# Two feature tiles per sigmoid, gate product, rounding and low part in the first mixer, with the second product four feature tiles behind

## Chip, cores and metric

The kernel runs as one program on 1 core of one Trainium2 chip. The metric is the device time of one execution in microseconds (us). A core has TensorE (PE; its weight loads are listed apart as PEld), VectorE (DVE), ScalarE (ACT), GpSimd (POOL) and SyncE (SP, which here only issues DMAs).

## What is computed

Three stages follow each other (4 batches, sequence length 768, model width 384 = 8 heads of 48):

```python
# attention: a state decayed in each step, per batch and head
cur = einsum('bhd,bhe->bhde', u * k_t, v_t)
y_t = einsum('bhd,bhde->bhe', r_t, state + cur)
state = w * state + einsum('bhd,bhe->bhde', k_t, v_t)
# first mixer: 384 -> 1024 -> 384, convolution of 3 taps over the sequence
h = maximum(x @ w_in, 0)
conv = sum over k of conv_w[k] * h shifted by k - 1
x = (h * sigmoid(conv)) @ w_out
# second mixer: 384 -> 1536 -> 384, with a norm in front
xn = (x - mean) / sqrt(var + 1e-6) * g_ln
out = x + maximum(xn @ w_ch1, 0) @ w_ch2
```

All operands are float32. Each large product is made of three products of rounded high parts (type fp32r) and low parts: high by high, high by low, low by high.

## The kernel before

**Attention** goes over 24 tiles of 128 sequence positions (`attn_tile`, line 341, and `state_update`, line 380). Its generator is advanced by `step()` (line 728). It delivers the transposed high and low parts `xh`, `xl` that the first mixer reads. The DMAs of a tile's inputs `rk`, `kt` and `rv` are issued by `load_tile` three tiles ahead, into buffers that earlier tiles have left. DVE multiplies `rk` by a table (line 347) before PE may use it.

**First mixer** (`mixer1`, line 539): 8 blocks of T = 384 positions, each with NF1 = 8 feature tiles of 128 features, so 64 feature tiles in all. For each of them `moe1_up` (line 463) makes:
- the first product, 9 matmuls of 386 columns into a `psm` bank (two banks);
- on ACT a relu into `h` (line 471) and the middle tap into `c` (line 472); on DVE the two outer taps into `c` (line 474, two instructions);
- for the feature tile before it (`prev`): `gate`, that is the sigmoid on ACT (line 454) and the product h * c on DVE (line 455), and then `gate_split`, the rounding to the high part `gh` on ACT (line 460) and the low part `gl` on DVE (line 461).

So sigmoid, product, rounding and low part are one instruction of 128x384 each per feature tile: 64 of each in the kernel.

**The second product** (`down`, line 441; 9 matmuls of 384 columns into three `acc` banks) is queued by `queue_down` and run by `pump(n)` until at most n are left in the queue. `LAG` is 3. In `mixer1` a feature tile's second product is queued one tile late and `pump(LAG - 1)` leaves two, so PE runs it right behind the first product three feature tiles on. The queue reaches over the end of a block: the last three second products of a block run in the next one, and those of the last block in the second mixer. After a block's eighth second product ACT empties the three `acc` banks (`evacuate`, line 496), and `spill` writes them to DRAM.

**Around it**: `before1` and `after1` (lines 762 and 768) put the decoding of the weights (`need`, `wdo`) and the attention's `step()` into the feature loop. A weight's high and low parts are made out of raw words by ACT, POOL and DVE. `need(wo_job[f - LAG + 1])` calls for the rows of the second weight that are to come.

**Second mixer** (`mixer2`, line 555): 6 blocks of 512 positions, 12 feature tiles each, with relu and low part only, and `pump(LAG)`.

**Order of the work**: the order on PE is the order in which the program is written (`InOrder`, line 67); so is the order of the weights' decoding among itself. The instructions of `v_`, `a_`, `g_` and the loads on SP are put in order, and the on-chip buffers put in place, when the program is built, by a planner with a timing model of its own (`_TILE`, line 851). Each engine then runs its instructions in that fixed order, and waits on semaphores.

Of the kernel before, what the change touches and what calls it, by code (L numbers as in the profile page):

```python
# [8 lines left out]
F32 = mybir.dt.float32  # L9
F32R = mybir.dt.float32r  # L10
I32 = mybir.dt.int32
AF = mybir.ActivationFunctionType
ALU = mybir.AluOpType
# [7 lines left out]
NF1 = FF1 // 128  # L21
NF2 = FF2 // 128
C = 128
TPB = S // C
NT = B * TPB
T = 384
TT = T // C
# [8 lines left out]
LAG = 3  # L36
# [12 lines left out]
def body(ctx, tc, r, k, v, w, u, w_in, conv_w, w_out, g_ln, w_ch1, w_ch2, rkT, krv, small, out):  # L49
# [6 lines left out]
    mp = ctx.enter_context(tc.tile_pool(name="mp", bufs=2))  # L56
# [6 lines left out]
    v_ = nc.vector  # L63
# [29 lines left out]
    gl = smallt[:, 3 * NP:]  # L93
# [347 lines left out]
    def down(acc, gh, gl_, wh, wl, f, nf):  # L441
        for t in range(len(acc)):
            sl = slice(t * 128, t * 128 + 128)
            for q, (a, x) in enumerate(((gh, wh), (gh, wl), (gl_, wh))):
                pe.matmul(acc[t], lhsT=a[:, sl], rhs=x, start=(f == 0 and q == 0),
                          stop=(f == nf - 1 and q == 2))
# [5 lines left out]
    def gate(st):  # L452

        a_.activation(out=st["c"], in_=st["c"], func=AF.Sigmoid)  # L454
        v_.tensor_tensor(out=st["c"], in0=st["h"][:, 1:T + 1], in1=st["c"], op=ALU.mult)  # L455

    def gate_split(st):
        st["gh"] = mp.tile([128, T], F32R, tag="gh", name="gh", bufs=LAG + 1)
        st["gl"] = mp.tile([128, T], F32R, tag="gl", name="gl", bufs=LAG + 1)
        a_.activation(out=st["gh"], in_=st["c"], func=AF.Copy)  # L460
        v_.tensor_tensor(out=st["gl"], in0=st["c"], in1=st["gh"].bitcast(F32), op=ALU.subtract)  # L461

    def moe1_up(x, f, prev):
        ps = ps_m.tile([128, 512], F32, tag="m", name="psm")
        mm3(ps[:, 0:T + 2], [wih[:, kt] for kt in range(KT)], [wil[:, kt] for kt in range(KT)], x[0], x[1], slice(f * 128, f * 128 + 128), slice(0, T + 2))
        if prev is not None:
            gate(prev)
        st = {}
        h = st["h"] = mp.tile([128, T + 2], F32, tag="h", name="h", bufs=3)
        c = st["c"] = mp.tile([128, T], F32, tag="c", name="c", bufs=3)  # L470
        a_.activation(out=h, in_=ps[:, 0:T + 2], func=AF.Relu)
        a_.activation(out=c, in_=h[:, 1:T + 1], func=AF.Copy, scale=cw[:, 1, f:f + 1])  # L472
        for tap, o in ((0, 0), (2, 2)):
            v_.scalar_tensor_tensor(out=c, in0=h[:, o:o + T], scalar=cw[:, tap, f:f + 1], in1=c,  # L474
                                    op0=ALU.mult, op1=ALU.add)
        if prev is not None:
            gate_split(prev)
        return st

    def moe2_up(xn, f, cols):  # L480
        ps = ps_m.tile([128, 512], F32, tag="m", name="psm")
        a, f0 = divmod(f * 128, WN)
        mm3(ps[:, 0:cols], c1h[a], c1l[a], xn[0], xn[1], slice(f0, f0 + 128), slice(0, cols))
        st = {}
        gh = st["gh"] = mp.tile([128, T2], F32R, tag="rh", name="rh", bufs=LAG + 1)
        gl_ = st["gl"] = mp.tile([128, T2], F32R, tag="rl", name="rl", bufs=LAG + 1)
        a_.activation(out=gh[:, 0:cols], in_=ps[:, 0:cols], func=AF.Relu)  # L487
        v_.scalar_tensor_tensor(out=gl_[:, 0:cols], in0=ps[:, 0:cols], scalar=0.0, in1=gh[:, 0:cols].bitcast(F32),  # L488
                                op0=ALU.max, op1=ALU.subtract)
        return st  # L490
# [35 lines left out]
    def pump(n):  # L526
        while len(downq) > n:
            downq.pop(0)()

    def queue_down(st, hold, f, nf, wh, wl, then, tiles=TT):  # L530
        def go():
            if f == 0:
                hold.extend(new_acc(tiles))
            down(hold, st["gh"], st["gl"], wh(f), wl(f), f, nf)
            if f == nf - 1:
                then(hold)
        downq.append(go)

    def mixer1(x, then, before=lambda f: None, after=lambda f: None):
        hold, prev = [], None  # L540
        for f in range(NF1):
            before(f)
            st = moe1_up(x, f, prev)
            if prev is not None:
                queue_down(prev, hold, f - 1, NF1, lambda f: woh[:, f, :], lambda f: wol[:, f, :], then)
            prev = st
            after(f)
            pump(LAG - 1)
            after(f)
        before(NF1)  # L550
        gate(prev)
        gate_split(prev)
        queue_down(prev, hold, NF1 - 1, NF1, lambda f: woh[:, f, :], lambda f: wol[:, f, :], then)

    def mixer2(xn, tiles, then, before=lambda f: None, after=lambda f: None):
        hold = []
        for f in range(NF2):
            before(f)
            queue_down(moe2_up(xn, f, tiles * C), hold, f, NF2, lambda f: c2h[f // 2][:, f % 2, :],
                       lambda f: c2l[f // 2][:, f % 2, :], then, tiles)  # L560
            pump(LAG)
            after(f)
# [315 lines left out]
```

## Time and profile before

| | us |
|---|---|
| median of 3 runs | 669.76 |
| lowest and highest of them | 665.53, 671.35 |
| the profiled execution, its own time | 668.53 |
| its span, from first to last instruction | 666.8 |
| PE, DVE, ACT, POOL busy in the span | 629.3, 431.7, 264.3, 135.1 |
| mean granted clock of TensorE, as a share of full speed | 0.976 |

The span lies 1.7 us below its execution's own time, and that time 1.2 us below the median. Busy time of PE is the time in which at least one matmul's record runs; records overlap. On DVE and ACT too the record of an instruction can reach over the start of the next one.

### The profile page before, as it was taken

The page shows a single profiled execution, that of the slowest core. Times are in us where ns is not written, and L with a number is a line of the kernel's source. Part 1 is how long each engine was busy: PE and PEld are TensorE (multiplying, and loading weights), DVE is VectorE, ACT ScalarE, POOL GpSimd, SP SyncE. Part 2 cuts the span into 40 slices and gives each one's busy share as a digit, 9 for nine tenths or more (in the row PEclk, how much of TensorE's full clock was granted, in tenths as well). Part 3 has the DMA queues.
Part 4 walks back from the last instruction along what each step waited for, and adds up shares of the span by engine and source line. Part 5 has one row for each costly group of instructions (what it writes and reads, how often), then busy time and mean ns, then how long its engine had stood idle before and what let it go on. Part 6 is the DMA issues. An engine that isn't in the chain of part 4 may idle for free.

```text
span 666.8 us, 11692 instructions
## 1 busy us (share of the span) xinstructions
PE 629.3 (94%) x4782; PEld 574.1 (86%) x4782; DVE 431.7 (65%) x772; ACT 264.3 (40%) x518; POOL 135.1 (20%) x142
## 2 busy tenths in 40 slices
PE   5879689999989899999999999999999999999996
PEld 4769579889879898899998999999999999999996
DVE  7887999999999998988788852422422422421211
ACT  3356656455654565566665521221211121121110
POOL 5374642230321213011007510100100100100000
PEclk9978799999989899999999999999999999999999
DMA  8663616235254434102043301101100200200101
GB/s 275 201 211 109 218 41 211 87 101 173 74 161 132 138 102 132 43 2 83 14 167 115 110 1 48 47 1 56 40 1 23 72 1 13 83 1 1 47 1 52
DMA packets 25294, 56.50 MB, mean 85 GB/s; under 512 B 2961, under 2 KB 15378, under 8 KB 25234
## 3 DMA queue, kind: packets, MB, share of 16 engines
q1 hardware_dynamic: 25234, 55.68, 26.3%
q8 instruction: 39, 0.64, 0.4%
q14 instruction: 21, 0.17, 0.1%
HBM read 46.24 MB, written 9.44 MB: 83 GB/s over the span
## 4 chain that ended last, share of the span: by engine, by line
PE 62%; DVE 24%; DMA 6%; issue 3%; ACT 3%; POOL 1%; SPq 1%; DVEq 0%; ACTq 0%
PE psm L75 30%; PE acc L75 30%; DVE c L474 6%; DMA rk<-in_rkT_dram 5%; DVE wdec L75 4%; DVE c L455 2%; DVE aT L363 2%; DVE rk L347 2%; DVE gl L461 2%; PE yps L75 1%; PE pxt L75 1%; DVE av L352 1%; DVE kks L249 1%; DVE a L354 1%; DVE xl L372 1%
## 5 line engine op out<-in xcount | busy, mean ns | idle before, releaser
L488 DVE SCALAR_TENSOR_TENSOR rl<-psm,rh 128x512 fp32r<-128x512 f32 x72 | 49.6, 689 | 133.0 <-ACT rh L487 129.5
L487 ACT ACTIVATE rh<-psm 128x512 fp32r<-128x512 f32 x72 | 43.1, 599 | 193.7 <-PE psm L75 190.1
L75 PE MATMUL acc<-c2h,rh 128*128 128x384 f32 x288 | 97.1, 337 | 0.0
L75 PE MATMUL acc<-c2l,rh 128*128 128x384 f32 x288 | 97.0, 337 | 0.0
L75 PE MATMUL acc<-c2h,rl 128*128 128x384 f32 x288 | 97.0, 337 | 0.0
L474 DVE SCALAR_TENSOR_TENSOR c<-h,tables,c 128x384 f32<-128x384 f32 x128 | 87.0, 685 | 7.4 <-ACT c L472 6.8
L75 PE MATMUL psm<-xnh,c1h 128*128 128x512 f32 x216 | 86.6, 401 | 0.0
L75 PE MATMUL psm<-xnh,c1l 128*128 128x512 f32 x216 | 84.9, 393 | 0.0
L75 PE MATMUL psm<-xnl,c1h 128*128 128x512 f32 x216 | 84.6, 392 | 0.0
L75 PE MATMUL psm<-xh,wih 128*128 128x386 f32 x192 | 70.0, 364 | 7.5 <-DVE aT L363 3.2
L75 PE MATMUL acc<-woh,gh 128*128 128x384 f32 x192 | 68.1, 355 | 2.7 <-ACT x L496 2.7
L75 PE MATMUL acc<-wol,gh 128*128 128x384 f32 x192 | 65.8, 343 | 4.2 <-DVE wol L75 4.2
L75 PE MATMUL psm<-xl,wih 128*128 128x386 f32 x192 | 67.4, 351 | 2.4 <-POOL xl L288 2.4
L75 PE MATMUL acc<-woh,gl 128*128 128x384 f32 x192 | 66.1, 344 | 1.8 <-DVE gl L461 1.8
L75 PE MATMUL psm<-xh,wil 128*128 128x386 f32 x192 | 67.3, 351 | 0.5 <-DVE wil L75 0.5
L75 POOL TENSOR_SCALAR wdec<-wdec 128x768 f32<-128x768 f32 (+2 forms) x19 | 55.3, 2911 | 50.8 <-ACT wdec L75 41.3
L511 POOL TENSOR_TENSOR rs<-rs,nhalf 128x1 f32<-128x1 f32 x24 | 15.5, 654 | 230.5 <-DVE rs L510 229.9
L75 PEld LDWEIGHTS acc<-c2l,rh 128*128 128x128 f32 x288 | 54.1, 188 | 3.0
L75 PEld LDWEIGHTS acc<-c2h,rh 128*128 128x128 f32 x288 | 54.1, 188 | 2.8
L75 PEld LDWEIGHTS acc<-c2h,rl 128*128 128x128 f32 x288 | 54.0, 188 | 0.0
L454 ACT ACTIVATE c<-c 128x384 f32<-128x384 f32 x64 | 33.4, 521 | 44.0 <-DVE c L474 43.5
L357 POOL TENSOR_SCALAR_AFFINE_SELECT aT<-a 128x1024 f32<-128x1024 f32 x18 | 29.1, 1617 | 104.0 <-PE yps L75 45.1
(115 smaller groups left out, 1144.2 us busy)
## 6 DMA issues: line engine op xcount, KB each, us to landing
rk<-in_rkT_dram SPq DMA_DIRECT2D x24, 448.0 KB, 5.0
st<-in_moe_w_ch_dram SPq DMA_DIRECT2D x12, 768.0 KB, 5.9
rv<-in_krv_dram SPq DMA_DIRECT2D x18, 448.0 KB, 4.8
kt<-in_krv_dram SPq DMA_DIRECT2D x24, 192.0 KB, 2.8
x_dram<-x SPq DMA_DIRECT2D x24, 192.0 KB, 2.0
x1b<-x_dram SPq DMA_DIRECT2D x24, 192.0 KB, 3.5
out_dram<-x1b SPq DMA_DIRECT2D x24, 192.0 KB, 2.3
st<-in_moe_w_in_dram SPq DMA_DIRECT2D x6, 512.0 KB, 6.1
```

Source lines behind the costliest of these rows:

```text
L75: return lambda *args, **kw: tc.keep_in_program_order(op(*args, **kw))
L249: v_.tensor_tensor(out=kks[:, n % 2, :, :, 0:D], in0=loaded[n][1].unsqueeze(1).to_broadcast([128, 2, H, D]), in1=tku, op=ALU.mult)
L347: v_.tensor_tensor(out=rk, in0=rk, in1=trk, op=ALU.mult)
L357: g_.affine_select(out=aT.rearrange("x q p c -> x (q p) c"), in_=a8.to_broadcast([128, H, C]), compare_op=ALU.is_equal, fill=0.0, base=0, ...
L363: v_.copy_predicated(out=aT[:, q], mask=later.bitcast(I32).unsqueeze(1).to_broadcast([128, NP, C]), data=dps[q])
L454: a_.activation(out=st["c"], in_=st["c"], func=AF.Sigmoid)
L455: v_.tensor_tensor(out=st["c"], in0=st["h"][:, 1:T + 1], in1=st["c"], op=ALU.mult)
L461: v_.tensor_tensor(out=st["gl"], in0=st["c"], in1=st["gh"].bitcast(F32), op=ALU.subtract)
L474: v_.scalar_tensor_tensor(out=c, in0=h[:, o:o + T], scalar=cw[:, tap, f:f + 1], in1=c, op0=ALU.mult, op1=ALU.add)
L487: a_.activation(out=gh[:, 0:cols], in_=ps[:, 0:cols], func=AF.Relu)
L488: v_.scalar_tensor_tensor(out=gl_[:, 0:cols], in0=ps[:, 0:cols], scalar=0.0, in1=gh[:, 0:cols].bitcast(F32), op0=ALU.max, op1=ALU.subtract)
L511: g_.tensor_tensor(out=rs[:, 1:2], in0=rs[:, 0:1], in1=nhalf, op=ALU.pow)
```

## The change

`h`, `c`, `gh` and `gl` become tiles of two feature tiles (`[128, 2, ...]`), three buffers of each (`gh` and `gl` had four of one). Relu and taps still go feature tile by feature tile, into their half. At every even feature tile the pair before it gets one sigmoid, one product, one rounding and one low part of 128x768, and its two second products are queued together. `pump` leaves three in the queue behind an even feature tile and two behind an odd one, so that a second product runs four feature tiles behind its first. `mixer2` is the same but for the form of the call.

```diff
     def gate(st):
 
         a_.activation(out=st["c"], in_=st["c"], func=AF.Sigmoid)
-        v_.tensor_tensor(out=st["c"], in0=st["h"][:, 1:T + 1], in1=st["c"], op=ALU.mult)
+        v_.tensor_tensor(out=st["c"], in0=st["h"][:, :, 1:T + 1], in1=st["c"], op=ALU.mult)
 
     def gate_split(st):
-        st["gh"] = mp.tile([128, T], F32R, tag="gh", name="gh", bufs=LAG + 1)
-        st["gl"] = mp.tile([128, T], F32R, tag="gl", name="gl", bufs=LAG + 1)
+        st["gh"] = mp.tile([128, 2, T], F32R, tag="gh", name="gh", bufs=3)
+        st["gl"] = mp.tile([128, 2, T], F32R, tag="gl", name="gl", bufs=3)
...
-    def moe1_up(x, f, prev):
+    def moe1_up(x, f, st, prev):
...
-        st = {}
-        h = st["h"] = mp.tile([128, T + 2], F32, tag="h", name="h", bufs=3)
-        c = st["c"] = mp.tile([128, T], F32, tag="c", name="c", bufs=3)
+        if not st:
+            st["h"] = mp.tile([128, 2, T + 2], F32, tag="h", name="h", bufs=3)
+            st["c"] = mp.tile([128, 2, T], F32, tag="c", name="c", bufs=3)
+        h, c = st["h"][:, f % 2], st["c"][:, f % 2]
...
     def mixer1(x, then, before=lambda f: None, after=lambda f: None):
-        hold, prev = [], None
+        hold, prev, st = [], None, None
+
+        def queue(f):
+            for q in range(2):
+                queue_down(prev["gh"][:, q], prev["gl"][:, q], hold, f + q, NF1, lambda f: woh[:, f, :],
+                           lambda f: wol[:, f, :], then)
+
         for f in range(NF1):
             before(f)
-            st = moe1_up(x, f, prev)
-            if prev is not None:
-                queue_down(prev, hold, f - 1, NF1, lambda f: woh[:, f, :], lambda f: wol[:, f, :], then)
-            prev = st
+            if f % 2 == 0:
+                prev, st = st, {}
+            moe1_up(x, f, st, prev if f % 2 == 0 else None)
+            if f % 2 == 0 and f:
+                queue(f - 2)
             after(f)
-            pump(LAG - 1)
+            pump(4-1 - f % 2)
             after(f)
         before(NF1)
+        prev = st
         gate(prev)
         gate_split(prev)
-        queue_down(prev, hold, NF1 - 1, NF1, lambda f: woh[:, f, :], lambda f: wol[:, f, :], then)
+        queue(NF1 - 2)
```

## Rows read from the trace of the kernel before

**Rows 1.** The page, part 2: busy tenths and clock in 40 slices.

```profile
PE   5879689999989899999999999999999999999996
...
DVE  7887999999999998988788852422422422421211
...
PEclk9978799999989899999999999999999999999999
```

**Rows 2.** Busy time by stage (the columns are named in its first line).

```profile
core 0: us, PE busy (x) PEld busy (x) DVE busy (x) ACT busy (x) POOL busy (x), PEclk, DMA share, GB/s
0.00:60.00 60.00, 45.65 (x538) 39.51 (x539) 47.44 (x86) 28.83 (x61) 32.06 (x60) 0.86 0.66 204
60.00:280.00 220.00, 202.69 (x2151) 183.39 (x2150) 211.43 (x344) 123.50 (x252) 64.38 (x52) 0.97 0.41 127
280.00:349.00 69.00, 69.00 (x499) 67.83 (x498) 55.17 (x112) 45.41 (x95) 5.84 (x5) 1.00 0.19 64
349.00:660.00 311.00, 311.00 (x1596) 282.65 (x1596) 116.10 (x230) 66.52 (x112) 32.81 (x26) 1.00 0.11 36
```

**Rows 3.** The chain of work that ended last, 60 to 280 us: shares by line.

```profile
by line: DVE c L474 17.7%; DMA rk<-in_rkT_dram 9.0%; DVE wdec L75 7.6%; issue 7.2%; DVE c L455 7.0%; DVE aT L363 7.0%; DVE gl L461 5.3%; DVE rk L347 5.1%; PE acc L75 4.9%; PE psm L75 4.7%; DVE av L352 2.9%; DVE kks L249 2.6%; DVE a L354 2.0
```

**Rows 4.** The same chain, 280 to 349 us: shares by line.

```profile
by line: PE psm L75 46.0%; PE acc L75 46.0%; PE yps L75 4.8%; PE pxt L75 1.9%; PE dps L75 1.6%
```

**Rows 5.** PE's waits, 60 to 280 us: in total, times, longest.

```profile
PE acc L75 <- DVE wol L75: 4.2, 2, 2.5
...
PE acc L75 <- DVE gl L461: 1.8, 2, 1.6
```

**Rows 6.** Groups of DVE instructions by shape, 60 to 280 us.

```profile
L455 DVE TENSOR_TENSOR c<-h,c 128x384 f32<-128x384 f32 x42 | 24.7, 587 | 1.1 <-ACT c L454 0.6
L461 DVE TENSOR_TENSOR gl<-c,gh 128x384 fp32r<-128x384 f32 x42 | 24.3, 580 | 0.5
```

**Rows 7.** Timeline of DVE around 308 us: start, duration.

```profile
308.04 0.55 DVE L461 TENSOR_TENSOR gl<-c,gh 128x384 fp32r<-128x384 f32 x1
308.51 0.95 DVE L75 TENSOR_TENSOR c2l<-wdec,c2h 128x768 fp32r<-128x768 f32 x1
309.38 0.55 DVE L455 TENSOR_TENSOR c<-h,c 128x384 f32<-128x384 f32 x1
309.85 0.61 DVE L474 SCALAR_TENSOR_TENSOR c<-h,tables,c 128x384 f32<-128x384 f32 x1
```

**Rows 8.** Groups of ACT instructions by shape, whole span.

```profile
L460 ACT ACTIVATE gh<-c 128x384 fp32r<-128x384 f32 x64 | 33.4, 522 | 35.2 <-DVE c L455 34.7
...
L75 ACT ACTIVATE c2h<-wdec 128x768 fp32r<-128x768 f32 x6 | 5.1, 847 | 7.5 <-DVE wdec L75 7.5
```

**Rows 9.** Pieces of the chain near 305 us: start, duration.

```profile
304.99 1.58 PE acc L75 x9
306.57 1.60 PE psm L75 x9
```

**Rows 10.** SP's waits, whole span.

```profile
SPq L737 <- ACT x L496: 105.7, 16, 30.8
```

**Rows 11.** Pieces of the chain, 60 to 300 us.

```profile
62.55 0.53 ACT gh L460
...
272.70 0.53 ACT c L454
```

**Rows 12.** DVE's waits, 60 to 280 us.

```profile
DVE rk L347 <- DMA rk<-in_rkT_dram: 5.5, 5, 1.8
```

**Rows 13.** Timeline around 317 us, DVE and PE: start, duration.

```profile
316.90 0.55 DVE L461 TENSOR_TENSOR gl<-c,gh 128x384 fp32r<-128x384 f32 x1
...
317.57 0.33 PE L75 MATMUL acc<-woh,gh 128*128 128x384 f32 x1
...
317.91 0.34 PE L75 MATMUL acc<-woh,gl 128*128 128x384 f32 x1
```

**Rows 14.** ACT's waits, whole span.

```profile
ACT rh L487 <- DVE rs L510: 3.6, 1, 3.6
```

More of the change, by code (lines that the diff above doesn't have):

```diff
@@ L477, in moe1_up @@
             gate_split(prev)
-        return st
     def moe2_up(xn, f, cols):
@@ L528, in pump, with queue_down @@
             downq.pop(0)()
-    def queue_down(st, hold, f, nf, wh, wl, then, tiles=TT):
+    def queue_down(gh, gl_, hold, f, nf, wh, wl, then, tiles=TT):
         def go():
@@ L533, in go @@
                 hold.extend(new_acc(tiles))
-            down(hold, st["gh"], st["gl"], wh(f), wl(f), f, nf)
+            down(hold, gh, gl_, wh(f), wl(f), f, nf)
             if f == nf - 1:
@@ L558, in mixer2 @@
             before(f)
-            queue_down(moe2_up(xn, f, tiles * C), hold, f, NF2, lambda f: c2h[f // 2][:, f % 2, :],
+            st = moe2_up(xn, f, tiles * C)
+            queue_down(st["gh"], st["gl"], hold, f, NF2, lambda f: c2h[f // 2][:, f % 2, :],
                        lambda f: c2l[f // 2][:, f % 2, :], then, tiles)
```

## The prediction

> **What bounds the kernel now.** I read the page's 40 slices first, to cut the run into stages [rows 1]: PE stands at 9 in most slices from about a sixth of the run on, and DVE at 9 only up to the middle. The busy times of each stage say which of the two sets the pace [rows 2]. From 60 to 280 us DVE works 211.43 of 220 us and PE 202.69, so PE idles 17.3 us there. From 280 to 349 us PE never idles, and DVE does 55.17 of 69. From 349 to 660, the second mixer, PE never idles and nothing of the change runs but the last few second products. The chain that ended last agrees: between 60 and 280 us DVE lines lead it and the two matmul groups of the mixer have 9.6% together [rows 3]; between 280 and 349 it is PE alone, 92% of it first and second product [rows 4]. So time that DVE is spared counts in the 220 us up to 280, time that PE loses counts from 280 on, and what ACT is spared counts hardly anywhere, as it works 123.5 of the 220 us [rows 2].
>
> **The change part by part.**
>
> *DVE, product and low part.* Per pair of feature tiles two products and two low parts of 384 become one of 768 each: 2 instructions fewer, or one per feature tile, 64 in all. What is one worth? Its record is 0.55 us, but the next instruction starts before the record ends. In the timeline a low part starts at 308.04 and the next instruction at 308.51, and the product takes 309.38 to 309.85: both hold DVE for 0.47 us. A subtraction of 768 starts at 308.51 and its successor at 309.38: 0.87 us [rows 7]. So two times 384 cost 0.94 and one times 768 costs 0.87, and a removed instruction gives 0.07 us. By the lengths of the records it would be 2 x 0.55 - 0.95 = 0.15 us. I take 0.07, since DVE is paid by when the next may start, and keep 0.15 for the range. In the stage that DVE sets there are 42 products and 42 low parts [rows 6], so 42 instructions go: 42 x 0.07 = 2.9 us gained (6.3 at the upper end). The other 22 go where PE is the bound or before the stage begins: nothing.
>
> The Trainium skill (VectorE: DVE Perf Modes, "The DRAIN you can't avoid") says that an operation does not start until the pipe of the one before is empty. By that rule the whole 0.15 us would be saved. The rows just read show a start 0.08 us ahead of the record's end, against it; the rule's result is the first rival below.
>
> *ACT, sigmoid and rounding.* A rounding of 384 has a record of 522 ns, a copy of 768 one of 847 [rows 8]: at most 0.2 us per removed instruction, 64 of them, 12.6 us in all. ACT has 96 us of idle time in the DVE-bound stage, so I count nothing. The cost is that of a longer single instruction: a relu behind the sigmoid of a pair starts 0.3 us later, every other tile, and the two `psm` banks cover that, as PE has a second product of 1.58 us between two first products [rows 9]. Without that cover it would be 32 x 0.3 = 10 us.
>
> *PE, one more feature tile behind.* The matmuls are the same. In the first block the first second product comes one feature tile later, and from there on each place in PE's order has one second product fewer behind it. At the end there are four instead of three left for the second mixer. One is 1.58 us [rows 9]. Up to 280 us PE idles anyway, so the missing work only makes a hole; from 280 on PE is full and does it on top: 1.6 us lost. The lower bound is 0, if waits of the second product on its weight's low part, 4.2 us in the stage [rows 5], go because it comes later while its decoding is called for at the same place. I take 1.6, since an earlier arrival on PE means only a wait on the next thing from DVE.
>
> *The wait on the paired result.* An even tile's result is ready only with its odd neighbour's, but its second product comes a tile later. For the odd one, the distance from the end of its first product to the second product of its pair's first half is six units of PE (three second, three first products), as it was before from an odd tile to its own. Within that distance the path grows: two ACT instructions by 0.3 and two DVE instructions by 0.40 each, 1.4 us. Behind a waiting matmul stands all of PE. In the DVE-bound stage that wait falls into idle time (1.8 us of such waits now [rows 5]); in the PE-bound stage it is a price. The tightest place there has a low part that runs from 316.90 to 317.45 and a matmul that reads it at 317.91 [rows 13], 0.46 us of slack. I count 0, as DVE has 14 us to spare in that stage and gets there earlier with fewer instructions; upper bound in the third rival.
>
> *Spill.* A block's eighth second product runs one feature tile later, so its emptying on ACT and its three DMAs do too. On SP the spills already wait 105.7 us in all for that [rows 10], with loads for the attention planned around them. Bounds: 0, or one unit pair of 3.2 us [rows 9] at each of the 5 waits of DVE on `rk` [rows 12], 16 us. I take 0, as the order on SP is planned anew and no load needs a spill until the last block. The three `acc` banks are emptied before the next block's first second product, with one first product between, as before.
>
> *Sum.* The profiled execution took 668.53 us: -2.9 + 1.6 gives 667.2. It lies 1.2 us below the median of the runs, 669.76, so on that scale the forecast is 668.4 us.
>
> **The rivals.**
>
> 1. *Each instruction's whole record counts.* Mechanism: DVE and ACT hand `c` and `gh` to each other, and where an engine waits for the other it pays the record's end too. For it: the chain from 60 to 280 has 11 pieces of sigmoid or rounding, 0.53 us each, standing between DVE pieces [rows 11]. Against it: back to back DVE shows 0.07 [rows 7], and it waits 8.6 us in all there. Worked out: 42 x 0.15 = 6.3; the 11 pieces become half as many of 0.85, -1.1; the 1.6 of PE goes into waits on weights. 668.53 - 7.4 = 661.1, or 662.3 on the median's scale.
>
> 2. *DVE's time is hidden.* The stage is then set by the ring "PE is done with `rk`, DMA, DVE, PE": `rk`'s DMA is 9.0% of the chain [rows 3] and DVE waits 5.5 us for it [rows 12]. Against it: DVE has only 8.6 us free of 220. Nothing is gained and the 1.6 is lost: 670.1, or 671.4.
>
> 3. *The pair comes too late for PE, and the kernel gets slower.* Place: the stage from 280 us, with some 10 pairs (20 feature tiles in 69 us at 3.2 each [rows 2, 9]). If the planner puts rounding and low part of a pair behind the next tile's taps, as it did before, the path of 1.4 us longer meets the slack of 0.46 [rows 13]: it decides from there. One such place costs 1.0; each of 10, 10 us. For it: that slack. Against it: DVE's spare 14 us. 668.53 - 2.9 + 1.6 + 10 = 677.2, or 678.5.
>
> 4. *Room.* The four tags grow from 21,528 to 36,912 bytes per partition by their shapes and counts, 15,384 more. Where tiles of different kinds share room, one waits for another. A relu of the second mixer now waits 3.6 us for a step of the norm that hands it nothing [rows 14], which may be such a case. Three of these: 667.2 + 10.8 = 678, or 679. No row shows how full the memory is. The Trainium skill (SBUF — State Buffer, Specifications) gives some 208 KiB usable per partition; no run here shows it.
>
> That the change doesn't do what it says I don't see: product and low part must show 32 records of 768.
>
> **How the numbers follow.** Forecast 0.45 (its own range 665 to 672), first rival 0.25, second 0.12, third 0.12, fourth 0.06. A measurement of this kernel can tell about 1%, 6.7 us, from no change: below 663.1 or above 676.5. Faster by over 1%: 0.7 of the first rival and a little of the forecast, 0.20. Slower by over 1%: 0.8 of the third and fourth and a little of the rest, 0.16. Within: 0.64. The range goes from 661, which holds most of the first rival, to 677, which leaves out the upper half of the third and most of the fourth.
>
> **What would show it right or wrong.** Right: DVE's products and low parts are 32 each at about 0.95 us, with 0.87 us from one start to the next; busy DVE falls by some 4 to 5 us; the stage that DVE sets ends 2 to 4 us earlier; PE's waits on `gl` stay under 4 us; the second mixer begins with two second products in a row and takes 1.6 us more. Wrong: waits of PE on `gh` or `gl` past 300 us (third rival); new waits between tiles that hand each other nothing (fourth); PE's idle time up to 280 unchanged (second) or down by 6 us or more (first). Above all the planner's new order on DVE and ACT may move the attention's instructions by more than all of this, in either direction.

## The result and the profile after

The changed kernel takes 672.29 us (median of 17 runs, 669.69 to 675.69), the kernel before 667.80 us beside it (17 runs, 665.44 to 671.35). The ratio is 1.0069, 95% interval 1.0053 to 1.0085: slower by 4.6 us (3.5 to 5.7), where 1.3 us less was forecast. The time lies in the range, but on the other side of the kernel before than the forecast.

The profiled execution took 671.24 us, with a span of 669.5; [rows 1] now read:

```profile
PE   5889689998999989999999999999999999999996
...
DVE  6879999999999889877798942422412422422211
...
PEclk9979789998999989999999999999999999999998
```

The picture is the same at this scale. The stages [rows 2], columns as there:

```profile
60.00:280.00 220.00, 201.67 (x2139) 184.55 (x2138) 210.09 (x303) 116.09 (x213) 67.36 (x52) 0.96 0.40 124
280.00:349.00 69.00, 69.00 (x496) 67.58 (x495) 53.77 (x91) 43.17 (x74) 6.81 (x5) 1.00 0.19 64
349.00:660.00 311.00, 310.19 (x1587) 280.58 (x1586) 116.73 (x225) 66.83 (x110) 30.54 (x26) 1.00 0.11 36
```

DVE issues 41 instructions fewer from 60 to 280 us, 303 for 344; 42 were counted. But in the same 220 us PE gets no more work done (201.67 us busy for 202.69), and in the second mixer PE now idles for 0.81 us. Groups of DVE instructions from 60 to 280 us [rows 6]:

```profile
L455 DVE TENSOR_TENSOR c<-h,c 128x768 f32<-128x768 f32 x20 | 20.5, 1026 | 3.7 <-ACT c L454 3.6
L461 DVE TENSOR_TENSOR gl<-c,gh 128x768 fp32r<-128x768 f32 x21 | 20.3, 968 | 0.3 <-ACT gh L460 0.2
```

Number and length are close to the forecast (1.03 and 0.97 us on average for 0.95). New is the end of the first line: ahead of the products DVE stands still for 3.6 us, waiting for the sigmoid; before it was 0.6 [rows 6]. The timeline of DVE shows the spacing [rows 7]:

```profile
345.27 0.95 DVE L455 TENSOR_TENSOR c<-h,c 128x768 f32<-128x768 f32 x1
346.13 1.94 DVE L508 BATCH_NORM_STATS2 bs<-x1b 128x6 f32<-128x384 f32 x4
```

The next instruction starts 0.86 us after the product, so a removed instruction gives 0.08 us here (2 x 0.47 - 0.86), 0.07 by forecast. By the rule of the Trainium skill that the prediction weighed (VectorE: DVE Perf Modes, "The DRAIN you can't avoid") it would start only when the pipe is empty, which the prediction took as the record's end, 0.95 us after; the trace is against that here too. The same section has an exception that the prediction left out: "A next op that is not held starts earlier". On ACT the groups of the whole span [rows 8] are

```profile
L454 ACT ACTIVATE c<-c 128x768 f32<-128x768 f32 x32 | 27.0, 843 | 43.2 <-DVE c L475 43.2
L460 ACT ACTIVATE gh<-c 128x768 fp32r<-128x768 f32 x32 | 27.0, 842 | 22.1 <-DVE c L455 22.1
```

so ACT works less, and a product waits for 0.84 us of sigmoid where it waited for 0.52. DVE's two longest kinds of wait from 60 to 280 us [rows 12] (total, times, longest):

```profile
DVE rk L347 <- DMA rk<-in_rkT_dram: 4.1, 5, 1.7
DVE c L455 <- ACT c L454: 3.6, 5, 0.9
```

PE's waits in that stage [rows 5]:

```profile
PE pst L75 <- DVE xl L372: 6.0, 5, 2.5
PE psm L75 <- ACT wih L75: 5.6, 1, 5.6
PE psm L75 <- DVE aT L363: 3.3, 2, 2.2
PE acc L75 <- DVE gl L461: 1.3, 1, 1.3
PE acc L75 <- DVE wol L75: 0.8, 1, 0.8
```

PE's waits on the weights' low part fell from 4.2 to 0.8 and those on `gl` stayed small; PE waits more for the attention and for the first weights (6.0 and 5.6; 1.7 and 3.0 before). SP's waits for the spill moved little (105.7 in [rows 10]):

```profile
SPq L746 <- ACT x L496: 101.8, 14, 30.5
```

Where the loss shows is in four rows of PE's timeline: the first matmul of the second mixer, the first of its second block, the first of its sixth, and the last matmul. Between them the program of the two kernels is the same, but for what was left over from the first mixer. Before:

```profile
348.99 0.39 PE L75 MATMUL psm<-xnh,c1h 128*128 128x512 f32 x1
...
398.82 0.40 PE L75 MATMUL psm<-xnh,c1h 128*128 128x512 f32 x1
...
604.48 0.39 PE L75 MATMUL psm<-xnh,c1h 128*128 128x512 f32 x1
...
660.66 0.33 PE L75 MATMUL acc<-c2h,rl 128*128 128x384 f32 x1
```

After:

```profile
347.47 0.39 PE L75 MATMUL psm<-xnh,c1h 128*128 128x512 f32 x1
...
400.07 0.40 PE L75 MATMUL psm<-xnh,c1h 128*128 128x512 f32 x1
...
606.48 0.39 PE L75 MATMUL psm<-xnh,c1h 128*128 128x512 f32 x1
...
662.77 0.34 PE L75 MATMUL acc<-c2h,rl 128*128 128x384 f32 x1
```

From the first of these rows to the last matmul it is 311.67 us before and 315.30 after: 3.63 us lost. Of these 2.77 go in the first block (49.83 to 52.60), 0.76 in blocks two to five (205.66 to 206.42) and 0.1 in the last. A second execution of each kernel (before_again, 666.87 us, and after_again, 671.96) gave 311.59 and 315.30, so this part is no scatter. The start of the second mixer scatters: 348.99 and 347.15 before, 347.47 and 348.32 after, so up to there nothing was gained that can be seen, where 2.9 was forecast.

The first block's 2.77 us can be read out. One more second product stands there, 1.58 us by [rows 9]. Most of the rest is this, on PE:

```profile
354.78 0.34 PE L75 MATMUL acc<-woh,gh 128*128 128x384 f32 x1
354.95 0.33 PE L75 MATMUL acc<-wol,gh 128*128 128x384 f32 x1
356.10 0.45 PE L75 MATMUL acc<-woh,gl 128*128 128x384 f32 x1 [0.81 <-DVE gl L461]
356.38 0.34 PE L75 MATMUL acc<-woh,gh 128*128 128x384 f32 x1
```

and at the same time on DVE:

```profile
353.24 1.94 DVE L75 SCALAR_TENSOR_TENSOR wdec<-st,wdec 128x768 int32<-128x768 int32 x2
355.09 0.95 DVE L461 TENSOR_TENSOR gl<-c,gh 128x768 fp32r<-128x768 f32 x1
```

The low part of the last pair ends at 356.04 and the matmul that reads it starts at 356.10. The one ahead of it started at 354.95, and such starts lie 0.17 us apart, so it is about 1.0 us late, with all of PE behind it. The chain that ended last, 280 to 349 us [rows 4], follows that wait back into DVE and ACT:

```profile
by line: PE psm L75 42.0%; PE acc L75 41.0%; PE yps L75 4.8%; DVE bs L508 2.2%; PE pxt L75 1.9%; DVE c L475 1.8%; PE dps L75 1.6%; DVE c L455 1.3%; DVE gl L461 1.2%; ACT c L473 0.9%; ACT h L472 0.7%; issue 0.6%; DVE mv L509 0.3%
```

First and second product have 83% there, 92% before.

### The profile page after: what moved, and what is told of

It is laid out like the page before. It is cut to its first block, busy times and chain, and to the rows that moved or that the text cites. A ratio compares the mean times of both kernels' runs of the same rounds, so it can differ in the third digit from the quotient of the medians.

```text
span 669.5 us, 11533 instructions
## 1 busy us (share of the span) xinstructions
PE 630.7 (94%) x4782; PEld 576.2 (86%) x4782; DVE 427.7 (64%) x708; ACT 254.6 (38%) x454; POOL 134.5 (20%) x142
## 4 chain that ended last, share of the span: by engine, by line
PE 63%; DVE 23%; DMA 5%; issue 4%; ACT 2%; POOL 2%; SPq 0%; DVEq 0%; ACTq 0%; POOLq 0%
PE acc L75 29%; PE psm L75 28%; DVE c L475 5%; DMA rk<-in_rkT_dram 5%; DVE wdec L75 3%; DVE aT L363 2%; DVE c L455 2%; PE yps L75 2%; DVE rk L347 2%; DVE gl L461 2%; PE dps L75 1%; PE pxt L75 1%; DVE av L352 1%; DVE kks L249 1%; PE pa L75 1%
## 5 line engine op out<-in xcount | busy, mean ns | idle before, releaser
L75 POOL TENSOR_SCALAR wdec<-wdec 128x768 f32<-128x768 f32 (+2 forms) x19 | 53.3, 2803 | 61.3 <-ACT wdec L75 56.7
L75 PEld LDWEIGHTS psm<-xnh,c1l 128*128 128x128 f32 x216 | 40.6, 188 | 9.5
L75 PEld LDWEIGHTS psm<-xh,wih 128*128 128x128 f32 x192 | 37.6, 196 | 11.7 <-ACT wih L75 5.9
```

The source lines that it names most:

```text
L75: return lambda *args, **kw: tc.keep_in_program_order(op(*args, **kw))
```

## The experiments

All ratios are to the kernel before, run on the same chip beside the kernel in question. "u2" is the start of the second mixer's first matmul, "u2 to last" the stretch from there to the start of the last matmul, both from the profiled execution.

### Distance, pairing and room, one at a time

**single_lag4**: the kernel before with its second product four tiles behind, nothing paired.

```diff
-        ... tag="gh", name="gh", bufs=LAG + 1)
+        ... tag="gh", name="gh", bufs=LAG + 2)
...
-            pump(LAG - 1)
+            pump(LAG)
```

(`gl` likewise.)

> The kernel before with the second product four feature tiles behind (three left in the queue instead of two, one more buffer for the high and the low part), without pairs. Theory A: one second product more in the PE-bound part, no DVE time saved: slower by 1.6 us, 1.002 to 1.004. Theory B: no change, 0.998 to 1.002, as the pairing is missing. Theory C: near 1.000, room grows by 3 KB per partition only.

Measured: 669.71 us, ratio 1.0028 (1.0005 to 1.0052). u2 at 349.68, u2 to last 313.49, which is 1.82 more than before; 1.55 of it lies in the second mixer's first block. The deferred second product costs what [rows 9] says, and the distance alone gains nothing ahead of u2: by the medians the kernel takes 1.9 us more in all. DVE's wait for the sigmoid, still of one feature tile, is longer from 60 to 280 us than the 0.6 of the kernel before:

```profile
DVE c L455 <- ACT c L454: 1.6, 2, 1.0
```

**pair_lag3**: the changed kernel at the old distance.

```diff
-            pump(4-1 - f % 2)
+            pump(LAG - 1 - f % 2)
```

> The changed kernel with the second product three feature tiles behind again: one fewer is left in the queue behind each feature tile, the pairing stays. Theory A (the pairing saves DVE time, the extra tile of distance costs one second product of 1.58 us and the late wait of 1.1 us at the start of the second mixer): faster than the changed kernel by 1.6 to 2.7 us, unless PE's waits on the low part in the PE-bound stage grow by as much; against the kernel before 0.995 to 1.002. Theory B (the pairing itself makes it slower, by the longer path or by a worse order on DVE and ACT): stays at 1.005 or goes over it, with PE's waits on the low part above 4 us. Theory C (room on the chip): as the changed kernel, near 1.007.

Measured: 692.29 us, ratio 1.0354 (1.0316 to 1.0391). PE's longest waits from 60 to 349 us:

```profile
PE acc L75 <- DVE gl L461: 12.2, 11, 2.5
PE acc L75 <- ACT gh L460: 8.9, 5, 2.5
```

That is Theory B's answer. Without the fourth tile of distance PE waits on the pair itself, and u2 comes at 372.33. From there to the last matmul it is 311.78, as before: the loss behind u2 belongs to the distance, not to the pairing.

**pair_spread**: the changed kernel, where the second mixer's first block runs its extra second product in the fourth feature tile and not in the first, so that two in a row don't meet the last pair.

```diff
-            pump(LAG)
+            pump(LAG + (more if f < 3 else 0))
```

(`more` is 1 in the first of the six blocks, else 0.)

> The changed kernel, but the second mixer's first three feature tiles leave one more in the queue, so that its first pass does not run two of the first mixer's second products in a row. Theory A: the wait of PE on the last pair's low part (0.8 us listed, 1.1 us of delay) goes, the deferred second product stays: faster than the changed kernel by some 1 us, near 1.005 of the kernel before. Theories B and C: no difference from the changed kernel, 1.007.

Measured: 670.41 us, ratio 1.0034 (1.0010 to 1.0057); u2 at 348.70, u2 to last 314.24, 1.06 less than in the changed kernel, and no wait on `gl` at that place. DVE's wait for the sigmoid is still 3.6 us up to 280 us. The 1.06 is sure, since this stretch repeats between executions to 0.1 us; that the median fell by 1.9 is not (see pair_product_late).

**single_room**: the kernel before with six buffers of `h`, `c`, `gh` and `gl`, by shapes and counts the bytes of the changed kernel.

```diff
-        h = st["h"] = mp.tile([128, T + 2], F32, tag="h", name="h", bufs=3)
+        h = st["h"] = mp.tile([128, T + 2], F32, tag="h", name="h", bufs=6)
```

(The other three tags likewise.)

> The kernel before with six buffers each of relu output, tap sum, high part and low part, so that these four take the bytes per partition that they take in the changed kernel, and nothing else. Theory C (room): slower, 1.004 to 1.008, with new waits between tiles that hand each other nothing. Theories A and B: within 0.998 to 1.002, or faster, since more buffers take waits away.

Measured: 667.88 us, ratio 1.0004 (0.9981 to 1.0027). The fourth rival falls.

### What DVE's time is worth

**lag4_tap_cut**: single_lag4, with the second outer tap on 116 of 384 columns (the other columns lack that tap).

```diff
-            v_.scalar_tensor_tensor(out=c, in0=h[:, o:o + T], scalar=cw[:, tap, f:f + 1], in1=c,
+            n = T - 268 if tap else T
+            v_.scalar_tensor_tensor(out=c[:, 0:n], in0=h[:, o:o + n], scalar=cw[:, tap, f:f + 1], in1=c[:, 0:n],
```

> Single feature tiles, second product four behind, and the second of the two outer taps works on 116 of its 384 columns, so that part of the convolution is left out. That spares DVE 268 columns, 0.28 us per feature tile, 11.7 us in the 42 tiles of the stage that DVE sets, four times what the pairing spares there, and makes no path longer. Theory A (DVE sets that stage's pace, and a microsecond spared counts as nearly one): 11.7 us below the same kernel with all columns (1.0028), that is 0.983 to 0.990. Theory D (time spared on DVE counts by half or less, as the ring over the DMA of rk and PE takes over): 0.994 to 0.999. Prediction's second rival (DVE's time is hidden): 1.000 to 1.004.

Measured: 662.65 us, ratio 0.9918 (0.9893 to 0.9943), 7.1 us below single_lag4 and between the ranges of Theories A and D. What one tap spares is read from DVE's timeline:

```profile
305.21 0.32 DVE L475 SCALAR_TENSOR_TENSOR c<-h,tables,c 128x116 f32<-128x116 f32 x1
305.45 0.55 DVE L461 TENSOR_TENSOR gl<-c,gh 128x384 fp32r<-128x384 f32 x1
...
308.22 0.61 DVE L475 SCALAR_TENSOR_TENSOR c<-h,tables,c 128x384 f32<-128x384 f32 x1
308.74 0.24 DVE L510 BATCH_NORM_AGGREGATE mv<-bs 128x2 f32<-128x6 f32 x2
```

A start to the next takes 0.24 us for 0.52, so 42 of them spare 11.8 us, and 7.1, six tenths, arrive at the end. DVE's time does set the stage, so the second rival falls, but not one for one. Part of what is spared turns into waiting: DVE's wait for the sigmoid, of one feature tile as in single_lag4, is 3.0 us here for 1.6 there.

**single_lag5** and **single_lag5to3**: the kernel before at distance five (`pump(LAG + 1)`, `bufs=LAG + 3`), and at five in blocks 0 to 3, four in block 4, three from block 5 on:

```diff
-            pump(LAG - 1)
+            pump(LAG - 1 + more)
...
-        mixer1(xT[j], spill(j), before1, after1)
+        mixer1(xT[j], spill(j), before1, after1, 2 if j < 4 else 1 if j == 4 else 0)
```

> The kernel before with the second product five feature tiles behind, without pairs. Theory A (each tile of distance leaves one second product of 1.58 us more for the part that PE bounds): 3.2 us, 1.004 to 1.006. Rival (the 1.0028 of four tiles was the planner's new order, not the distance): within 0.999 to 1.003.

> Single feature tiles; the second product runs five feature tiles behind in blocks 0 to 3, four in block 4 and three from block 5 on, so that nothing more than before is left for the part that PE bounds. Theory E (a longer distance lets the DVE-bound stage end some us earlier, 4.7 in the one profile with five, and each tile of distance that is left at its end costs one second product of 1.58 us in the second mixer): the end of the first mixer's first products stays 1.5 to 4.7 us before that of the kernel before and nothing is paid later, 0.993 to 0.998. Rival (the earlier end is the same work put off, which comes back whenever it is done): 0.999 to 1.002.

Measured: 668.68 us, 1.0014 (1.0002 to 1.0027), with u2 at 344.28 and u2 to last 314.98; and 667.89 us, 0.9993 (0.9979 to 1.0006), with u2 at 347.98 and u2 to last 311.58. The first forecast is missed: distance five costs 0.9 us and not 3.2, inside the rival's range. Behind u2 it takes the 3.3 us more that were forecast, but u2 comes 2.9 to 4.7 us earlier, which distance four didn't show. The second run gives its rival's answer: where the two second products are caught up in time, nothing is left of the earlier u2, so it was work put off. Why distance four shows the cost in full and five doesn't is open. A kernel with a larger distance is therefore to be read by u2 and by the stretch behind it together.

### Which of the paired instructions costs

Both of these have the spread of pair_spread. **pair_split_only** makes sigmoid and product feature tile by feature tile again, the even tile's one tile early, and pairs rounding and low part:

```diff
-        a_.activation(out=st["c"], in_=st["c"], func=AF.Sigmoid)
-        v_.tensor_tensor(out=st["c"], in0=st["h"][:, :, 1:T + 1], in1=st["c"], op=ALU.mult)
+        st, q = st
+        a_.activation(out=st["c"][:, q], in_=st["c"][:, q], func=AF.Sigmoid)
+        v_.tensor_tensor(out=st["c"][:, q], in0=st["h"][:, q, 1:T + 1], in1=st["c"][:, q], op=ALU.mult)
```

**pair_gate_only** pairs sigmoid and product and makes the other two tile by tile:

```diff
-        a_.activation(out=st["gh"], in_=st["c"], func=AF.Copy)
-        v_.tensor_tensor(out=st["gl"], in0=st["c"], in1=st["gh"].bitcast(F32), op=ALU.subtract)
+        for q in range(2):
+            a_.activation(out=st["gh"][:, q], in_=st["c"][:, q], func=AF.Copy)
+            v_.tensor_tensor(out=st["gl"][:, q], in0=st["c"][:, q], in1=st["gh"][:, q].bitcast(F32), op=ALU.subtract)
```

> Four tiles behind, spread at the second mixer's start; sigmoid and product again once per feature tile, rounding and low part once per pair. Half of the DVE time is spared that the full pairing spares (1.5 us in the stage). Theory A with the wait of the product for the paired sigmoid (3.6 us of DVE's idle time against 0.6 before) as what takes the saving back: that wait falls to 1.6 us or less, and the time is at or below that of the full pairing with the same spread, 1.000 to 1.0035. Rival (the paired rounding and low part, late for PE, are what costs): 1.004 or more, with PE's waits on the low part above 3 us.

> Four tiles behind, spread; sigmoid and product once per pair, rounding and low part once per feature tile, both of a pair's in the same place. Theory A: the wait of the product for the paired sigmoid stays at 3 to 4 us, half of the DVE time is spared, so 1.003 to 1.005, above the kernel that pairs rounding and low part only. Rival: at or below 1.002.

Measured: 669.29 us, 1.0022 (1.0001 to 1.0042), u2 at 345.37; and 671.48 us, 1.0055 (1.0032 to 1.0077), u2 at 349.05. Both ran beside the same executions of the kernel before, on one chip. Where sigmoid and product are paired, u2 comes 3.7 us later; behind u2 both take the same (315.22 and 315.06). The intervals of the two ratios overlap. DVE's wait for the sigmoid is 3.6 us in pair_gate_only, as expected. In pair_split_only it is

```profile
DVE c L456 <- ACT c L455: 2.6, 4, 0.8
```

and not the 1.6 or less that was expected. So the order of the two kernels is Theory A's, and the listed wait explains 1.0 us of the 3.7.

**pair_lag5**: the changed kernel at distance five, to give the pair more room.

```diff
-            pump(4-1 - f % 2)
+            pump(5-1 - f % 2)
```

(And `bufs=4` of `gh` and `gl`, with the two extra second products spread over the second mixer's first block.)

> Pairs as in the changed kernel, the second product five feature tiles behind, and the second mixer's first feature tiles leave more in the queue (two, then one). Theory F (at four tiles the path that the pair lengthens takes the spared DVE time back in the DVE-bound stage; with one tile more it does not): 2 to 3 us below the single tiles at the same distance (1.0014), 0.997 to 0.999. Rival (the pairing spares nothing that the chip can use, whatever the distance): 1.001 or more.

Measured: 672.11 us, 1.0061 (1.0038 to 1.0085); u2 at 345.79, u2 to last 316.10. DVE's wait for the sigmoid is 3.4 us. More distance doesn't help: PE has no wait on the pair here, and the time stays. The theory that asked for it falls.

**pair_product_late**: pair_spread with the pair's product written behind the next tile's taps, so that DVE has work during the long sigmoid.

```diff
     def gate(st):
...
-        v_.tensor_tensor(out=st["c"], in0=st["h"][:, :, 1:T + 1], in1=st["c"], op=ALU.mult)
...
+        v_.tensor_tensor(out=st["c"], in0=st["h"][:, :, 1:T + 1], in1=st["c"], op=ALU.mult)
         a_.activation(out=st["gh"], in_=st["c"], func=AF.Copy)
```

> pair_spread with one edit more: the product of a pair is issued on DVE behind the two taps of the next feature tile instead of ahead of them. It leaves DVE something to do while ACT makes the sigmoid of 768. If the wait for the paired sigmoid (3.6 us in the stage up to 280 us, 0.6 before) is what takes the DVE time back that the change spares, that wait falls below 1 us, the second mixer starts 1 to 2 us earlier than in pair_spread, and the ratio to before is 1.000 to 1.002. If the later product delays the low part as much as it spares, or the spared time is lost to other waits, the wait falls but the ratio stays at 1.003 or more.

Measured: 672.74 us, 1.0079 (1.0048 to 1.0109). But DVE's waits up to 280 us are

```profile
DVE rk L347 <- DMA rk<-in_rkT_dram: 6.0, 5, 2.3
DVE c L459 <- ACT c L454: 3.6, 5, 0.9
```

The planner orders DVE by its own model, not by where a line stands, and put every instruction of every engine where pair_spread has it. So the run says nothing on the wait. It says something else: one program gave 1.0034 (12 runs) and, on another chip, 1.0079 (6 runs), 2.3 us apart in the median. A difference of that size between two kernels measured on different chips shows nothing by itself.

**pair_sigmoid_single**: the changed kernel with the sigmoid alone made per feature tile; product, rounding and low part stay paired.

```diff
-        a_.activation(out=st["c"], in_=st["c"], func=AF.Sigmoid)
-        v_.tensor_tensor(out=st["c"], in0=st["h"][:, :, 1:T + 1], in1=st["c"], op=ALU.mult)
+        st, q = st
+        a_.activation(out=st["c"][:, q], in_=st["c"][:, q], func=AF.Sigmoid)
+        if q:
+            v_.tensor_tensor(out=st["c"], in0=st["h"][:, :, 1:T + 1], in1=st["c"], op=ALU.mult)
...
-            moe1_up(x, f, st, prev if f % 2 == 0 else None)
+            moe1_up(x, f, st, prev if f % 2 == 0 else None, (st, 0) if f % 2 else (prev, 1) if f else None)
```

> The changed kernel with the sigmoid alone made feature tile by feature tile again, the even tile's at the odd one and the odd one's at the next even one; product, rounding and low part stay paired. ACT has the time; DVE's instructions are the same as in the changed kernel. If the sigmoid of 768 ahead of the product is what takes DVE's spared time back, DVE's wait for the sigmoid in the stage up to 280 us falls from 3.6 us below 2, the second mixer starts 1 to 2 us earlier than in the changed kernel and the ratio to before is 1.003 to 1.006. If it is not, the wait may fall, but the ratio stays at 1.006 or more.

Measured: 668.02 us, 1.0014 (0.9993 to 1.0035); u2 at 345.28, u2 to last 315.47. DVE's waits and the busy times from 60 to 280 us, each in a fence of its own (columns as in [rows 12] and [rows 2]):

```profile
DVE c L457 <- ACT c L455: 2.0, 3, 0.8
DVE rk L347 <- DMA rk<-in_rkT_dram: 1.4, 3, 0.5
```

```profile
60.00:280.00 220.00, 204.03 (x2162) 186.08 (x2161) 214.08 (x308) 122.90 (x238) 69.51 (x52) 0.97 0.40 127
```

Against the changed kernel, the same paired DVE instructions now fill 214.08 of the 220 us for 210.09, and PE does 2.4 us more. Its two waits fell from 7.7 to 3.4 us, and the second mixer starts 2 to 3 us earlier. Of that, the wait for the sigmoid gave 1.6; it is at 2.0, just not below the 2 that was expected. The wait for `rk` gave 2.7, but it differs by as much between two executions of the kernel before (5.5 and, in before_again, 2.7), so it can't be put down to the edit. ACT has more work than before the edit, 122.90 for 116.09, and it doesn't matter. The ratio is lower than expected; the intervals of the two ratios, 1.0069 (1.0053 to 1.0085) and this one, don't overlap. The clock doesn't separate the two kernels: the mean granted clock over all their executions is 0.981 and 0.980.

**pair_sigmoid_single_spread**: the same, with one second product more kept in the queue during the second mixer's first feature tile.

```diff
-            pump(LAG)
+            pump(LAG + (more if f < 1 else 0))
```

> pair_sigmoid_single, and in the second mixer's first feature tile the queue keeps one second product more, so that the two in a row come one first product later. What the wait of PE on the last pair's low part at the second mixer's start costs (1.1 us in the changed kernel) goes; the deferred second product (1.6) and the slower matmuls of the second mixer (0.8) stay. Expected from the parts: 1 us less than pair_sigmoid_single, ratio 0.998 to 1.001, so no kernel that clearly beats the one before. If the parts don't add, because the planner's order for the first mixer comes out another way, the ratio is 1.002 or more.

Measured: 668.20 us, 1.0002 (0.9986 to 1.0018); u2 at 344.20, u2 to last 315.46. The ratio is in the expected range, but not for the expected reason: the wait on `gl` at the second mixer's start is 0.5 us for 0.6, so one feature tile is too little, and u2 to last is unchanged. The version is as fast as the kernel before, not faster.

### The unchanged matmuls that got slower

From block two to block six the second mixer takes 206.42 us in the changed kernel and 205.66 before, with the same 1,056 matmuls. All of it is in the first products: over 432 of them, the trace gives 235.8 ns from one start to the next, 233.3 before (1.1 us in all; the rest of these blocks is 0.3 us shorter). In three kernels on-chip tiles lie elsewhere, and by the names of operations and tiles the traces show on every engine the same sequence as in the kernel that each was made from: **single_c1_padded** leaves 64 bytes free behind each tile of the second mixer's first weights, **single_c1_joined** and **pair_c1_joined** make one tile of three.

```diff
-    c1h = [[big.tile([128, WN], F32R, name=f"c1h{a}{kt}") for kt in range(KT)] for a in range(FF2 // WN)]
+    c1h = [[big.tile([128, WN + 16], F32R, name=f"c1h{a}{kt}")[:, 0:WN] for kt in range(KT)] for a in range(FF2 // WN)]
```

(`c1l` likewise. The joined form:)

```diff
+    c1ht = [big.tile([128, KT, WN], F32R, name=f"c1h{a}") for a in range(FF2 // WN)]
+    c1h = [[c1ht[a][:, kt] for kt in range(KT)] for a in range(FF2 // WN)]
```

> The kernel before with 64 bytes of unused room behind each tile of the second mixer's first weights, so that these tiles lie at other addresses, and no instruction differs. If the place of the weights is what makes the second mixer's unchanged matmuls slower in the changed kernel, the mean from start to start of its first products leaves the 233.3 ns of before, towards the 235.8 of after or in the other direction by as much. If the place doesn't matter, it stays within 0.6 ns of 233.3.

> The kernel before with the second mixer's first weights in one tile per half of the columns instead of three, so that these and other tiles lie elsewhere. The same two answers: near 233.3 ns from start to start of the second mixer's first products if place doesn't matter, over 1 ns away if it does.

> The changed kernel with the second mixer's first weights in one tile per half of the columns. If the place of these weights makes its matmuls slower, the mean from start to start moves away from 235.8 ns by over 1; if the slower matmuls come from something else of the paired kernel, it stays between 235.2 and 236.4.

Measured, from the same two rows of PE's timeline as above, single_c1_padded:

```profile
396.87 0.39 PE L75 MATMUL psm<-xnh,c1h 128*128 128x512 f32 x1
...
602.92 0.39 PE L75 MATMUL psm<-xnh,c1h 128*128 128x512 f32 x1
```

single_c1_joined:

```profile
396.75 0.40 PE L75 MATMUL psm<-xnh,c1h 128*128 128x512 f32 x1
...
603.76 0.39 PE L75 MATMUL psm<-xnh,c1h 128*128 128x512 f32 x1
```

That is 206.05 and 207.01 us, or 234.8 and 236.7 ns from start to start, for 205.66 and 233.3 before. pair_c1_joined has 236.6, 0.8 from the changed kernel's 235.8, which is between its two answers. In the two single kernels the pace of these matmuls changes, by 1.5 and 3.4 ns, where the changed kernel lost 2.5, with nothing changed but where tiles lie, as far as the traces show. Other builds have other numbers still: 233.8 in single_lag4, 235.4 in pair_spread. Which places are good wasn't found, and that the changed kernel lost its 0.8 us this way fits but isn't shown. (One execution each: 667.09, 668.82 and 676.46 us; the last one's u2 is 351.95.)

## Why the prediction was wrong

**DVE, product and low part: nothing speaks against the term, and something else took it.** Where the sigmoid is not paired, u2 comes at 345.28 (pair_sigmoid_single), 344.20 (the same, spread) and 345.37 (pair_split_only, where only the low part is paired on DVE). The kernel before gave 348.99 and 347.15, single_room 347.68. Against their mean that is 2.7, 3.7 and 2.6 us, in single executions, which for one program differ by 1.8. The medians can be asked as well: what a kernel takes longer than the kernel before, less what it takes longer behind u2. That gives 2.9, 3.7 and 2.1 us gained ahead of u2, each give or take 1.4, and 0.0 for single_lag4. Forecast were 2.9, and 1.5 for the low part alone. With a paired sigmoid, u2 comes at 347.5 to 352.0 in the five kernels at distance four, and by the medians between 0.3 gained and 2.7 lost. The medians themselves lie apart too: 668.0 to 669.3 without a paired sigmoid, 670.4 to 672.7 with it (pair_lag5 among these). The 2.3 us between two measurements of one program make that gap less sharp but don't close it, since no kernel of one kind lies among the other.

**The step that failed** is "ACT, sigmoid and rounding": "ACT has 96 us of idle time in the DVE-bound stage, so I count nothing. The cost is that of a longer single instruction". I looked for the one who waits behind a longer sigmoid on ACT, a relu, and on PE, and put the rest at nothing; what the runs show is DVE waiting at the product, in the stage where DVE is the bound. With the sigmoid of 768 that listed wait is 3.6 us, in every kernel with a paired sigmoid at distance four, and 0.6 in the kernel before. ACT's idle time doesn't cover a latency: a busy engine that needs the result next pays it. [Rows 11] showed these pieces of sigmoid on the chain, between DVE pieces, and I took them only as a gain for the first rival. The same reading fails in "The wait on the paired result", which added up the longer path for PE alone.

That the pairing of the sigmoid takes back what DVE spares is shown: with it undone and DVE's instructions left as they are, the ratio goes from 1.0069 to 1.0014, and u2 comes 2 to 3 us earlier. That the listed wait is all of it is not shown. Of the 3.0 us by which it grew, 1.0 came with the distance alone (single_lag4 has 1.6), and with the sigmoid single and the low part paired it is still 2.0 and 2.6. So 1.0 to 2.0 us of wait belong to the sigmoid's pairing, less than the 2 to 4 us at u2. The rest, in other waits or in the order that the planner makes anew with every edit, stays open.

**PE, one more feature tile behind: right at this distance.** 1.6 was forecast; single_lag4 shows 1.55 in the second mixer's first block and 1.82 in all. At distance five the same reckoning gave 3.2 and 0.9 was measured, so it is no rule.

**The pair too late for PE: right mechanism, wrong place, one instead of ten.** From 280 us to the second mixer PE doesn't wait on `gl` at all, as the forecast had it. But the text said "the second mixer begins with two second products in a row" and priced only their work. Two in a row leave out the first product that gave the pair its time, so the odd tile meets a low part that DVE had put behind two steps of the decoding: 1.06 us by pair_spread. That the third rival's price of one place, 1.0, comes out is luck: it was 1.4 us of longer path less 0.46 of slack, and the delay found here comes from the two steps of the decoding.

**Spill, room: nothing**, as counted; single_room gave 1.0004. The second rival's reading "nothing is gained and the 1.6 is lost" comes nearest in its sum, for another reason: DVE's time wasn't hidden (lag4_tap_cut gave 7.1 us); what the pairs spared was taken back where the sigmoid was paired.

**Sum.** Forecast -2.9 + 1.6. Found: about 0 up to u2, +1.6, +1.06, +0.8 for the slower matmuls and 0.2 in small parts, 3.6 us from the profile. The medians say 4.6 (3.5 to 5.7). About 1 us has no place in the profile, less than what one program differs by between two measurements, and stays open. pair_sigmoid_single checks the account: -2.7 and +3.8 behind u2 give +1.1, measured 0.9. That the time lies inside the stated range of 661 to 677 is no merit of the sum: the range's upper part was there for the third and fourth rivals.

The remark at the prediction's end, that a new order on DVE and ACT may move more than all of this, was a fair warning but no term: it should have widened the forecast's own range of 665 to 672 upwards.

## What to carry to other kernels

Joining two instructions saves time on both engines of a chain (here about 0.07 us on DVE and 0.2 us on ACT for each instruction less), but the joined producer is a longer latency for whoever reads it next (0.84 us of sigmoid for 0.52). If that reader is the busy engine, leave apart the instruction that it waits for, as pair_sigmoid_single did with the sigmoid; product, rounding and low part stayed paired. That kernel is as fast as the kernel before and not faster: pairs need the fourth tile of distance (without it 692.29 us), and what that costs behind u2 is about what DVE spares. When a queue gets longer, look at where it is drained: there two units come in a row, and the last one meets data with less time ahead of it than anywhere else.

## What was not expected of the hardware

The pace of a chain of identical matmuls is not the same in every build: 233.3, 234.8 and 236.7 ns from start to start in three builds of the kernel before that, by the names of operations and tiles, run the same sequence on every engine; the edits change only where tiles lie. A build repeats its number: 233.3 and 235.8 came out twice each. Over 648 such matmuls 3.4 ns are 2.2 us, half of what the change cost. What about the place makes the difference isn't shown.

One program, with the same order on each engine, was measured at ratios of 1.0034 and 1.0079 on two chips, with intervals that overlap only from 1.0048 to 1.0057.
